# Attention and feed-forward on one core: another table of instruction order, buffer slots written out, three streamed parts of w2 in place of four

## The chip, the cores and the metric

The kernel runs on one core of a Trainium2 chip. The metric is device time in microseconds (us). Five engines run side by side, each through its own list of instructions in order: TensorE (PE, matrix products into PSUM), VectorE (DVE), ScalarE (ACT), GpSimd (POOL) and SyncE (SP), which here only issues DMA transfers. Engines wait for one another by semaphores.

## What is computed

The reference, cut to what matters: attention with random features, and then a two-layer network with an ELU between the layers.

```python
# q, k, v: [8, 8, 576, 64]; omega: [128, 64]
def phi(x):
    proj = np.einsum('bhsd,md->bhsm', x, omega)
    h = proj - np.sum(x * x, axis=-1, keepdims=True) / 2.0
    h = h - np.max(h, axis=-1, keepdims=True)
    return np.exp(h) / np.sqrt(m)
q_p, k_p = phi(q * scale), phi(k * scale)
kv, z = np.einsum('bhsm,bhsd->bhmd', k_p, v), np.sum(k_p, axis=2)
num = np.einsum('bhsm,bhmd->bhsd', q_p, kv)
den = np.einsum('bhsm,bhm->bhs', q_p, z)[..., None] + 1e-06
x = (num / den).transpose(0, 2, 1, 3).reshape(4608, 512)
h = x @ w_in                                      # w_in: 512 x 2048
g = np.where(h > 0.0, h, np.exp(np.minimum(h, 0.0)) - 1.0)
out = g @ w_out                                   # w_out: 2048 x 512
```

The weights arrive as 64-bit floats, and the kernel converts them on the chip.

## The kernel before

**Tiling.** The heads are taken two at a time, 32 pairs. For each pair the kernel loads k, q and v, projects them (`project`: the products `ppk` and `ppq`), takes minima and exponentials (`hk`, `hq`), sums k against v (`kv`), divides by the denominators (`finish`: `pz`, `den`) and multiplies (`output` or `visit`: `pn`, `pc`). The first 8 pairs are read by feature and squared on the chip (`square` in `project`); q and k of the later pairs come in a mixed layout. The tokens are nine blocks of 512. Blocks 0 and 1 run the first layer as plain products (`layer1`, tiles `ph`), in the order block 0 first half, block 1 first half, block 0 second half, block 1 second half, 32 steps F in all; while they run, the weights w1 and w2 are converted (`from_f64`, tiles `raw_w`, `u_w`) and combined (`combine`, tiles `tz`). Blocks 2 to 8 run the first layer two steps at a time as seven products in place of eight (`quad`: `pha`, `phb`, reading `w1q` tiles from memory and operands such as `A11x` or `S2x`). The second layer is `layer2` (tiles `acc`, from activations `g`, `ga`, `gb`). Numbers in a tile's name are the pair or the step F, and last a number of the buffer's.

**Visits.** For pairs 8 and up, `visit` puts the outputs of two pairs and the k-v sums of two other pairs into one stretch on PE. The sums and the last 64 tokens share one PSUM tile `pc`; ACT copies it to `zs` (L844), PE turns it (`pkt`, L847), and ACT or DVE copies that to `kvf`.

**Order.** Each operation is a numbered task of `Plan`, with the tiles that it reads and writes. `ORDER` is a table with the place of every task and, where a task may run on two engines, which one. `issue` writes the instructions in this order, so it sets each engine's list. A task of SP or ACT that issues a transfer waits in its list until its buffer is free; whatever stands behind it on that engine waits too.

**Buffers.** A tile (`Buf`) takes a buffer of its kind when its first task is issued. `SLOTS` has the number of buffers of a kind; all PSUM tiles share the kind `pa`, eight banks. w2 has 16 parts. Those named in `STREAMED` are converted once, stored to memory (`w2s`) and loaded again for each of the nine blocks into one single buffer (`w2`); the others stay in on-chip memory (`w2r`). The third piece of each `w1q` (768 KB) also has one single buffer, `w1b`; the first two pieces share three buffers.

Of the kernel before, what the change touches and what calls it, by code (L numbers as in the profile page):

```python
# [74 lines left out]
STREAMED = (3, 7, 11, 15)  # L75
# [6 lines left out]
def room(tag):  # L82
    return SLOTS[tag]
# [27 lines left out]

ORDER = """
# [189 lines left out]
class Buf:  # L302


    def __init__(self, pool, shape, dtype, tag, name, n):
        self.args, self.key, self.n = (pool, shape, dtype, name), tag, n
        self.tile, self.left, self.slot, self.listed, self.waits = None, 0, None, False, False
# [1313 lines left out]
```

## Time and profile before

| | us |
|---|---|
| median of 3 runs | 994.19 (992.09 to 994.51) |
| the profiled execution's own time | 994.99 |
| its span, first to last instruction | 992.9 |
| TensorE busy in the span | 970.7 (98%) |
| VectorE busy | 776.7 (78%) |
| ScalarE busy | 709.5 (71%) |
| GpSimd busy | 403.0 (41%) |

The profiled execution is 0.8 us above the median; 2.1 us of its time lie outside its span. Products are pipelined and the profile models their ends, so that a share of 98% leaves out short waits between products.

### The profile page before, as it was taken

What the parts mean: (1) busy time and instruction counts of PE and PEld (TensorE: products, weight loads), DVE (VectorE), ACT (ScalarE), POOL (GpSimd) and SP (SyncE); (2) the same over time, 40 slices, a digit from 0 to 9 for tenths busy, and PEclk for the clock granted to TensorE, in tenths of its full rate; (3) what the DMA queues carried; (4) which work ended last, traced back from release to release, by engine and by line L of the source; (5) the groups of instructions that cost most, each with busy time, mean ns of one, the idle gap of its engine ahead of it and who ended that gap; (6) DMA issues with size and microseconds to landing.
All of it is one profiled execution on the core that took longest, in us unless ns stands there. A gap on an engine that the chain in (4) does not pass through costs nothing.

```text
span 992.9 us, 20069 instructions
## 1 busy us (share of the span) xinstructions
PE 970.7 (98%) x6237; PEld 842.0 (85%) x6237; DVE 776.7 (78%) x2709; ACT 709.5 (71%) x1856; POOL 403.0 (41%) x382
## 2 busy tenths in 40 slices
PE   8999989999999999999999999999999999999998
PEld 7787768888778988988889988898899889898897
DVE  5999999999999978997889778787888565455343
ACT  5888867878899867896789779876998633333232
POOL 3544122245546542642555535745464322122120
PEclk8999999999999999999999999999999999999999
DMA  6767887879889888897888987887787767656763
GB/s 175 197 211 244 281 272 265 285 268 291 293 282 353 280 281 263 276 292 236 254 282 292 301 273 254 275 283 270 246 301 234 249 209 255 201 202 211 238 196 109
DMA packets 90697, 252.71 MB, mean 255 GB/s; under 512 B 11680, under 2 KB 24800, under 8 KB 90592
## 3 DMA queue, kind: packets, MB, share of 16 engines
q1 hardware_dynamic: 89648, 249.11, 77.5%
q10 hardware_dynamic: 944, 2.33, 0.8%
q8 instruction: 51, 0.84, 0.3%
q14 instruction: 54, 0.44, 0.1%
HBM read 206.83 MB, written 44.56 MB: 253 GB/s over the span
## 4 chain that ended last, share of the span: by engine, by line
PE 76%; DVE 8%; ACT 4%; DMA 3%; issue 2%; POOL 1%; DVEq 0%; ACTq 0%; POOLq 0%
PE acc L1415 35%; PE phb L1358 16%; PE pha L1358 12%; PE ppk L681 2%; PE ppq L681 2%; PE pn L817 2%; DMA w1q<-w1p 1%; PE ph L1303 1%; PE ph L1305 1%; PE ph L1304 1%; DMA xq<-in_qx_dram 1%; DVE e L1316 1%; DVE u_w L1157 1%; DVE g L490 1%; DVE u_w L1162 1%
## 5 line engine op out<-in xcount | busy, mean ns | idle before, releaser
L1415 PE MATMUL acc<-w2r,ga 128*128 128x512 f32 x504 | 136.4, 396 | 0.0
L1415 PE MATMUL acc<-w2r,gb 128*128 128x512 f32 x504 | 134.8, 395 | 0.0
L1415 PEld LDWEIGHTS acc<-w2r,ga 128*128 128x128 f32 x504 | 90.4, 189 | 16.9 <-issue 0.7
L1415 PEld LDWEIGHTS acc<-w2r,gb 128*128 128x128 f32 x504 | 90.3, 189 | 16.1
L490 POOL TENSOR_TENSOR gb<-e,gb 128x512 fp32r<-128x512 f32 x35 | 45.3, 1293 | 112.4 <-DVE gb L487 53.4
L901 DVE CUSTOM_DVE_ANT_0 junk<-hq,pz 128x128 f32<-128x128 f32 (+1 forms) x320 | 78.1, 282 | 8.9 <-PE pz L880 2.8
L690 ACT ACTIVATE p2q<-ppq,sqq 128x128 f32<-128x128 f32 x216 | 66.8, 369 | 23.3 <-PE ppq L681 17.2
L690 ACT ACTIVATE p2k<-ppk,sqk 128x128 f32<-128x128 f32 x216 | 66.4, 367 | 22.7 <-PE ppk L681 21.6
L490 POOL TENSOR_TENSOR ga<-e,ga 128x512 fp32r<-128x512 f32 x34 | 44.0, 1293 | 83.0 <-DVE ga L487 51.5
L1415 PE MATMUL acc<-w2r,g 128*128 128x512 f32 x288 | 74.5, 396 | 1.5 <-DVE mnk L699 1.2
L1387 ACT ACTIVATE e<-pha 128x512 f32<-128x512 f32 x56 | 33.5, 599 | 56.2 <-PE pha L1358 43.0
L1388 ACT ACTIVATE e<-e 128x512 f32<-128x512 f32 x112 | 70.4, 633 | 2.4
L582 ACT ACTIVATE hq<-hq,mnq 128x128 f32<-128x128 f32 x216 | 68.6, 397 | 0.2
L582 ACT ACTIVATE hk<-hk,mnk 128x128 f32<-128x128 f32 x216 | 67.8, 401 | 0.2 <-DVE mnk L699 0.2
L1367 DVE TENSOR_TENSOR phb<-phb,s 128x512 f32<-128x512 f32 x56 | 38.9, 695 | 35.1 <-PE phb L1358 34.8
L490 POOL TENSOR_TENSOR hq<-hq,den 128x512 f32<-128x512 f32 (+1 forms) x62 | 51.7, 843 | 35.8 <-DVE den L910 10.2
L699 DVE CUSTOM_DVE_ANT_0 hq<-ppq,p2q 128x128 f32<-128x128 f32 x216 | 53.1, 285 | 15.9 <-ACT p2q L690 13.9
L1415 PEld LDWEIGHTS acc<-w2r,g 128*128 128x128 f32 x288 | 52.4, 188 | 13.4 <-ACT e L1313 1.3
L490 POOL TENSOR_TENSOR tk<-xk,tk 64x576 fp32r<-64x576 f32 x33 | 47.2, 1429 | 40.6 <-DMA turned<-tb 10.0
L490 POOL TENSOR_TENSOR tq<-xq,tq 64x576 fp32r<-64x576 f32 x30 | 42.9, 1431 | 48.2 <-DVE tq L487 7.6
L699 DVE CUSTOM_DVE_ANT_0 hk<-ppk,p2k 128x128 f32<-128x128 f32 x216 | 53.1, 284 | 9.5 <-ACT p2k L690 8.4
L1390 DVE SCALAR_TENSOR_TENSOR e<-e,phb 128x512 f32<-128x512 f32 x56 | 38.2, 682 | 23.7 <-ACT e L1388 23.3
(266 smaller groups left out, 2747.6 us busy)
## 6 DMA issues: line engine op xcount, KB each, us to landing
w1q<-w1p SPq DMA_DIRECT2D x112, 512.0 KB, 5.6
w1q<-w1p SPq DMA_DIRECT2D x56, 768.0 KB, 5.5
w<-w2s SPq DMA_DIRECT2D x36, 512.0 KB, 5.9
raw_w<-in_w_dram SPq DMA_DIRECT2D x28, 512.0 KB, 4.6
xk<-in_kx_dram SPq DMA_DIRECT2D x24, 576.0 KB, 4.9
xq<-in_qx_dram SPq DMA_DIRECT2D x24, 576.0 KB, 5.5
turned<-tb SPq DMA_DIRECT2D x48, 288.0 KB, 4.2
qh<-turned SPq DMA_DIRECT2D x96, 144.0 KB, 6.0
```

The lines of the kernel that those rows point to most:

```text
L490: (nc.vector if e == "DVE" else nc.gpsimd).tensor_tensor(*args)
L582: nc.scalar.activation(h()[:, j, :], src(j), AF.Exp, bias=mn()[:, j:j + 1], scale=-1.0)
L681: nc.tensor.matmul(p()[:, a * 256:(a + 1) * 256], y()[:, o:o + P], om, start=True, stop=True)
L690: nc.scalar.activation(p2()[:, a], view()[:, a, M:], AF.Identity, bias=sq()[:, j:j + 1], scale=1.0)
L699: nc.vector.tensor_tensor_reduce(out=h()[:, j, :], in0=view()[:, a, 0:M], in1=p2()[:, a, :], scale=1.0, scalar=HIGHEST, op0=ALU.add, op1=A ...
L901: nc.vector.tensor_tensor_reduce(out=junk()[r], in0=h()[r, j, :], in1=pz()[r, a * P:(a + 1) * P], scale=1.0, scalar=EPS, op0=ALU.mult, op1 ...
L1358: nc.tensor.matmul(half(p, n), a, b, start=(first and c == 0 and i == 0), stop=(c == 1 and i == 2), skip_group_check=True,)
L1367: op("DVE", dve(n), d, lambda: nc.vector.tensor_tensor(out(), p(), x(), ALU.add), reads, writes)
L1387: op("ACT", act(TB, True), d1, lambda p=p, e=e: nc.scalar.activation(e(), p(), AF.Relu, scale=-1.0), (p,), (e,))
L1388: op("ACT", act(TB), d1 + 0.2, lambda e=e: nc.scalar.activation(e(), e(), AF.Exp, scale=-1.0), (e,), (e,))
L1390: "DVE", dve(TB), d1 + 0.8, lambda p=p, e=e: nc.vector.scalar_tensor_tensor(e(), e(), -1.0, p(), ALU.add, ALU.max),
L1415: nc.tensor.matmul(now[tt](), part_of(tt, a), w(), start=(first and n == 0), stop=(last and n == 2))
```

## The change

A new `ORDER` table; a table `SLOT` beside it, from which each tile takes the number of its buffer when its first task is ordered, where before the framework gave out the buffers of a kind in turn. Three parts of w2 are streamed, numbers 4, 9 and 15, where it was four, 3, 7, 11 and 15. The room for the thirteenth resident part comes from the tile `xc_1_3`, which now shares the buffer `w1b` with the third pieces of `w1q`. Scratch tiles `junk` become two fixed ones. The first four loads of w1 (`ASIDE`) are issued by SP, not ACT. The task costs in `op` (693 for 687 and the like) take no part in the instructions.

```diff
-STREAMED = (3, 7, 11, 15)
+STREAMED = (4, 9, 15)
...
+SLOT = """
+001010071600504023401376500203411710026275123007410026510131031140710000264621421031050561104270134020063072543111256031114035102022310063120421000143
...
 ORDER = """
-0 44 52 48 8 12 56 36 77 40 4 276 142 66 72 96 297 280 301 1004 108 100 112 144 148 68 172 176 80 84 288 152 16 104 20 284 60 500 88 24 1140 496 1008
...
+44 52 0 56 8 40 280 73 4 36 48 276 288 1004 60 284 12 96 140 69 144 66 160 148 100 104 300 78 172 152 156 176 180 1008 108 112 116 297 80 84 164 328
...
     def __call__(self):
         if self.tile is None:
             pool, shape, dtype, name = self.args
-            self.tile = pool.tile(shape, dtype, tag=self.key, bufs=self.n, name=name)
+            self.tile = pool.tile(shape, dtype, tag=self.key + self.slot, bufs=1, name=name)
         return self.tile
...
+        slots = iter("".join(SLOT.split()))
         for x in map(int, ORDER.split()):
             n, e = divmod(x, 4)
+            for b in sorted(self.tasks[n][4], key=lambda b: b.args[3]):
+                if b.slot is None:
+                    b.slot = next(slots)
...
+    junks = [const.tile([P, M], F32, name=f"junk{i}") for i in range(2)]
...
-        (blk, c): Buf(stream, [P, 2, TB], F32R, xc_tag(blk, c), f"xc_{blk}_{c}", room(xc_tag(blk, c)))
+        (blk, c): Buf(mv if xc_tag(blk, c) == "w1b" else stream, [P, 2, TB], F32R, xc_tag(blk, c), f"xc_{blk}_{c}", room(xc_tag(blk, c)))
...
-    ASIDE = ("w1_0", "w1_1", "w1_2", "w1_3")
+    ASIDE = ()
```

**The start.** SP's first issues stood so before (`xk` and `xq` are k and q of a pair, in pieces; `omf` is omega):

```order
L546 DMA xk_98<-in_k_dram 64x2x256
L546 DMA xq_100<-in_q_dram 64x2x512
L546 DMA xk_98<-in_k_dram 64x2x64
L546 DMA xq_100<-in_q_dram 64x2x64
L546 DMA xk_98<-in_k_dram 64x2x128
L546 DMA xk_116<-in_k_dram 64x2x512
L546 DMA xk_116<-in_k_dram 64x2x64
L546 DMA xq_152<-in_q_dram 64x2x64
L502 DMA omf<-in_omT_dram 64x128 x2
L546 DMA xq_152<-in_q_dram 64x2x512
L546 DMA v_164<-in_v_dram 128x650
```

and stand so now:

```order
L569 DMA xk_99<-in_k_dram 64x2x256
L569 DMA xq_101<-in_q_dram 64x2x512
L569 DMA xq_101<-in_q_dram 64x2x64
L569 DMA xk_107<-in_k_dram 64x2x64
L569 DMA xk_99<-in_k_dram 64x2x128
L569 DMA xk_99<-in_k_dram 64x2x64
L569 DMA xk_107<-in_k_dram 64x2x512
L569 DMA xq_120<-in_q_dram 64x2x64
L1162 DMA raw_w_1_122<-in_w_dram 128x1024
L569 DMA v_124<-in_v_dram 128x650
L569 DMA xq_120<-in_q_dram 64x2x512
```

The 64-column piece of the first q moved from fourth to third. The load `raw_w_1` of w1 now stands here, ninth. Before, ACT issued it, as the first rows of ACT's list show (L1522 loads its tables, L606 squares, L582 takes exponentials):

```order
L1522 ACT_TABLE_LOAD
L493 DMA of<-in_omT_dram 64x128
L544 DMA xk_98<-in_k_dram 64x2x128
L606 ACTIVATE xk_98<-xk_98 64x2x256
L1139 DMA raw_w_1_129<-in_w_dram 128x1024
L606 ACTIVATE xq_100<-xq_100 64x576
```

ACT's list now begins so:

```order
L1545 ACT_TABLE_LOAD
L516 DMA of<-in_omT_dram 64x128
L567 DMA xk_99<-in_k_dram 64x2x128
L629 ACTIVATE xq_101<-xq_101 64x576 x2
L605 ACTIVATE hk_149<-ppk_1_128,mnk_147 128x128 x4
L629 ACTIVATE xk_107<-xk_107 64x576
```

ACT squares both halves of q first; the square of the first 256 columns of k went from ACT to POOL.

**The end of block 2's first layer.** PE's products between the last use of the third piece `w1q_44_2` and the first use of the next one, `w1q_46_2`, before (the last 12 rows ahead of that first use; ahead of them stand three products of `ppk`, six of `acc` and the twelve of A11 and S2 of step 46):

```order
L1415 MATMUL acc_2_0_0_4053<-w2_43_5001,gb_42_4941 128x512
L1415 MATMUL acc_2_0_1_4039<-w2_43_5001,gb_42_4941 128x512
L1415 MATMUL acc_2_0_0_4053<-w2r_85,ga_44_5091 128x512 x2
L1415 MATMUL acc_2_0_1_4039<-w2r_85,ga_44_5091 128x512 x2
L681 MATMUL ppq_16_1_5102<-om_79,tq_16_4801 128x256 x2
L1358 MATMUL phb_46_5125<-S3x_2_3583,w1q_46_1_4865 128x256 x6
L1358 MATMUL phb_46_5125<-S1x_2_3801,w1q_46_1_4865 128x256 x6
L681 MATMUL ppq_16_0_5139<-om_79,tq_16_4801 128x256 x2
L1415 MATMUL acc_2_0_0_4053<-w2r_85,ga_44_5091 128x512
L1415 MATMUL acc_2_0_1_4039<-w2r_85,ga_44_5091 128x512
L1415 MATMUL acc_2_0_0_4053<-w2r_85,gb_44_5113 128x512 x2
L1415 MATMUL acc_2_0_1_4039<-w2r_85,gb_44_5113 128x512 x2
```

and now (ahead of them stand the twelve products of A11 and S2 of step 46, and nothing else):

```order
L1438 MATMUL acc_2_0_0_3915<-w2r_87,gb_42_4730 128x512
L1438 MATMUL acc_2_0_1_3886<-w2r_87,gb_42_4730 128x512
L1438 MATMUL acc_2_0_0_3915<-w2r_87,ga_44_4912 128x512 x2
L1438 MATMUL acc_2_0_1_3886<-w2r_87,ga_44_4912 128x512 x2
L1381 MATMUL phb_46_4928<-S3x_2_3304,w1q_46_1_4926 128x256 x6
L1381 MATMUL phb_46_4928<-S1x_2_3653,w1q_46_1_4926 128x256 x6
L1438 MATMUL acc_2_0_0_3915<-w2r_87,ga_44_4912 128x512
L1438 MATMUL acc_2_0_1_3886<-w2r_87,ga_44_4912 128x512
L1438 MATMUL acc_2_0_0_3915<-w2r_87,gb_44_4953 128x512 x2
L1438 MATMUL acc_2_0_1_3886<-w2r_87,gb_44_4953 128x512 x2
L704 MATMUL ppq_16_0_4973<-om_79,tq_16_4659 128x256 x2
L704 MATMUL ppq_16_1_4981<-om_79,tq_16_4659 128x256 x2
```

Three products of `ppk` and six of `acc` left this stretch: it held 24 products `phb` or `pha`, 18 of `acc` and seven of `ppk` and `ppq`, and now holds 24, 12 and four. On SP, ahead of the load of `w1q_46_2` stand the two stores `turned3` in both; behind it stood six fetches `qh` and the load `w2_47` before, and now five `qh`, a load of `w1q_48_0` and then `w2_47`.

**A visit.** ACT's list around the two copies `zs` in the visit of pairs 16 to 19, before:

```order
L485 CAST tq_20_6428<-xq_20_6382 64x576
L582 ACTIVATE hq_19_6251<-hq_19_6251,mnq_19_6252 128x128 x5
L844 COPY zs_19_6367<-pc_(16, 17)_(18, 19)_6393 128x128
L485 COPY xf_5_0_6459<-pn_17_6396 128x256
L844 COPY zs_18_5833<-pc_(16, 17)_(18, 19)_6393 128x128
L485 COPY xf_4_0_4889<-pn_17_6396 128x256
L485 COPY xf_5_0_6459<-pn_16_6390 128x256
L485 COPY xf_4_0_4889<-pn_16_6390 128x256
L485 CAST gb_58_6491<-e1_58_6384 128x512
L650 ACTIVATE xq_20_6382<-xq_20_6382 128x576
```

and DVE's list around its own copy out of the same PSUM tile `pc`:

```order
L901 ISA den_19_6451 128x1
L901 ISA junk_19_6_0_6455,den_19_6451<-hq_19_6251,pz_19_6431 128x128
L901 ISA den_19_6451 128x1
L901 ISA junk_19_7_1_6457,den_19_6451<-hq_19_6251,pz_19_6431 128x128
L901 ISA den_19_6451 128x1
L487 COPY xf_5_0_6459<-pc_(16, 17)_(18, 19)_6393 128x2x64
L910 RECIPROCAL den_19_6451<-den_19_6451 128x4
```

ACT's list now:

```order
L1410 ACTIVATE e1_58_6235<-phb_58_6063 128x512
L1411 ACTIVATE e1_58_6235<-e1_58_6235 128x512
L605 ACTIVATE hq_19_6056<-hq_19_6056,mnq_19_6057 128x128 x4
L508 CAST gb_58_6246<-e1_58_6235 128x512
L508 COPY xf_5_0_6248<-pn_17_6186 128x256
L867 COPY zs_18_5680<-pc_(16, 17)_(18, 19)_6183 128x128
L867 COPY zs_19_6217<-pc_(16, 17)_(18, 19)_6183 128x128
L508 COPY kvf1_81<-pkt_19_6264 128x128
L508 COPY xf_5_0_6248<-pn_16_6180 128x256
L673 ACTIVATE xq_21_6299<-xq_21_6299 128x576
L508 COPY xf_4_0_4742<-pn_16_6180 128x256
L1394 COPY s_60_6316<-pha_60_6271 128x256
```

and DVE's now:

```order
L513 TENSOR_TENSOR tq_20_6237<-xq_20_6139,tq_20_6237 64x576
L1413 SCALAR_TENSOR_TENSOR e1_58_6235<-e1_58_6235,phb_58_6063 128x512
L510 COPY xf_5_0_6248<-pc_(16, 17)_(18, 19)_6183 128x2x64
L817 TENSOR_TENSOR zr_19_6233<-zs_19_6217,zr_19_6233 128x256
L510 COPY xf_4_0_4742<-pn_17_6186 128x256
L510 CAST tq_20_6237<-xq_20_6139 64x576
L924 ISA junk0_82,den_19_6285<-hq_19_6056,pz_19_6252 64x128
```

DVE's copy out of `pc` went from behind four denominators to straight behind the add of step 58. ACT's two copies `zs` now follow each other. On PE the step 60 product `pha` follows `pkt` directly before; now four products of `acc` stand between them. In the visit of pairs 24 to 27 ACT's copy of `kvf0` stood behind four exponentials `hq_27` and a copy of `pn`; now it stands straight behind the copies `zs`.

**Choice of engines.** Over the whole program DVE has 5 instructions fewer, POOL 9 fewer and ACT 10 more. The larger moves: roundings `g` (block 0 and 1) on ACT 27 to 32, output copies `o` on ACT 24 to 28, squares of q on ACT 9 to 13, subtractions `tz` on DVE 8 to 14, normalisations `hq` on DVE 34 to 29. PE's 5649 instructions are the same ones in another order.

## Rows read from the trace of the kernel before

**Rows 1.** Busy time of each engine (instructions) by stretch, granted clock, DMA
```profile
core 0: us, PE busy (x) PEld busy (x) DVE busy (x) ACT busy (x) POOL busy (x), PEclk, DMA share, GB/s
0.00:25.00 25.00, 20.25 (x137) 19.55 (x138) 14.10 (x44) 15.00 (x44) 8.04 (x13) 0.86 0.66 176
25.00:150.00 125.00, 115.88 (x709) 93.69 (x708) 116.66 (x374) 102.89 (x274) 47.54 (x45) 1.00 0.77 242
150.00:300.00 150.00, 148.80 (x769) 120.75 (x768) 142.59 (x466) 128.29 (x326) 60.38 (x61) 1.00 0.84 282
300.00:975.00 675.00, 671.46 (x4565) 596.65 (x4564) 498.89 (x1821) 458.35 (x1208) 285.77 (x263) 1.00 0.80 258
```

**Rows 2.** What TensorE waited for, whole run: total us, times, longest
```profile
PE ppq L626 <- ACT xq L606: 2.4, 1, 2.4
...
PE pha L1358 <- DMA w1q<-w1p: 1.4, 1, 1.4
...
PE pha L1358 <- ACT kvf L485: 0.8, 1, 0.8
...
PE pkt L847 <- ACT zs L844: 0.6, 1, 0.6
```

**Rows 3.** Chain of work over 0 to 150 us: start, us, what
```profile
74.67 1.04 ACT hq L582 x4
...
118.90 0.68 DVE mnq L639
```

**Rows 4.** Timeline of the start: start, us, engine, operation, idle before
```profile
2.94 0.60 SPq L546 DMA_DIRECT2D xq<-in_q_dram  x1
...
3.79 0.36 ACTq L1139 DMA_DIRECT2D raw_w<-in_w_dram  x1
...
5.54 0.75 DVE L490 TENSOR_TENSOR xq<-xq 64x576 f32<-64x576 f32 x1 [2.51 <-DMA xq<-in_q_dram]
...
8.98 0.68 ACT L606 ACTIVATE xq<-xq 64x576 f32<-64x576 f32 x1 [4.56 <-DMA xq<-in_q_dram]
...
9.71 2.08 PE L626 MATMUL ppq<-of,xq 128*128 128x128 f32 x8 [2.39 <-ACT xq L606]
...
10.61 2.24 POOL L490 TENSOR_TENSOR xk<-xk 64x576 f32<-64x576 f32 x2 [4.06 <-DMA xk<-in_k_dram]
```

**Rows 5.** Busy time by stretch around the half clock, columns as above
```profile
10.00:15.00 5.00, 5.00 (x25) 5.00 (x25) 3.62 (x9) 2.69 (x9) 2.24 (x2) 0.50 0.79 225
15.00:20.00 5.00, 5.00 (x46) 5.00 (x46) 4.62 (x9) 4.54 (x19) 2.25 (x2) 0.99 0.82 217
```

**Rows 6.** DMA issues: count, KB each, median us to landing
```profile
w1q<-w1p SPq DMA_DIRECT2D x56, 768.0 KB, 5.5
...
xq<-in_q_dram SPq DMA_DIRECT2D x8, 32.0 KB, 3.2
```

**Rows 7.** Chain of work over 370 to 392 us
```profile
379.21 9.12 DMA w1q<-w1p
```

**Rows 8.** Chain of work over 825 to 860 us, TensorE alone
```profile
829.86 2.88 PE phb L1358 x24
...
833.46 4.20 PE acc L1415 x18
```

**Rows 9.** Timeline of ACT near 476 us
```profile
476.32 0.27 ACT L844 COPY zs<-c_(16, 17)_(18, 19)_6393 128x128 f32<-128x128 f32 x1 [1.53 <-DVE xf L487]
```

**Rows 10.** Timeline of ACT near 685 us
```profile
685.01 1.30 ACT L582 ACTIVATE hq<-hq,mnq 128x128 f32<-128x128 f32 x4
```

**Rows 11.** Groups of ACT: count, busy us, mean ns, idle before
```profile
L485 ACT CAST g<-e 128x512 fp32r<-128x512 f32 x27 | 16.8, 624 | 7.2 <-DVE e L1316 4.9 <-PE acc L1415 1.6 <-POOL g L490 0.7
...
L485 ACT COPY o<-acc 128x512 f32<-128x512 f32 x24 | 14.0, 595 | 18.9 <-PE acc L1415 16.5 <-DVE ga L490 1.5 <-POOL tz L490 0.7
```

**Rows 12.** Groups of DVE, columns as above
```profile
L490 DVE TENSOR_TENSOR hq<-hq,den 128x512 f32<-128x512 f32 x22 | 15.5, 705 | 0.2
...
L490 DVE TENSOR_TENSOR tz<-tw,tz 128x512 fp32r<-128x512 f32 x8 | 5.5, 688 | 0.2 <-ACT tz L485 0.2
```

More of the change, by code (lines that the diff above doesn't have):

```diff
@@ L306, in __init__ @@
         self.args, self.key, self.n = (pool, shape, dtype, name), tag, n
-        self.tile, self.left, self.slot, self.listed, self.waits = None, 0, None, False, False
+        self.tile, self.left, self.slot = None, 0, None
     def __call__(self):
@@ L497, in omega @@
         )
-        t = Buf(sb, [P, M], F32, "junk", "omf", 2)
+        t = Buf(sb, [P, 2, M], F32, "p2", "omf", 2)
         due += 15
@@ L501, in omega @@
             r = slice(a * D, a * D + D)
-            op("SP", 590, due, lambda r=r: nc.sync.dma_start(t()[r], omT), (), ((t, a),), D * M * 4)
+            op("SP", 590, due, lambda r=r: nc.sync.dma_start(t()[r, 0], omT), (), ((t, a),), D * M * 4)
         op(
-            "DVE", dve(M, True), due + 2, lambda: nc.vector.tensor_scalar(t(), t(), -SCALE, None, ALU.mult),
+            "DVE", dve(M, True), due + 2, lambda: nc.vector.tensor_scalar(t()[:, 0], t()[:, 0], -SCALE, None, ALU.mult),
             ((t, 0), (t, 1)), ((t, 0), (t, 1)), port=True,
         )
-        op("DVE", dve(M), due + 3, lambda: nc.vector.tensor_copy(om[:, 0:M], t()), ((t, 0), (t, 1)), ("oh",))
+        op("DVE", dve(M), due + 3, lambda: nc.vector.tensor_copy(om[:, 0:M], t()[:, 0]), ((t, 0), (t, 1)), ("oh",))
         op(
             "DVE", dve(M), due + 4,
-            lambda: nc.vector.tensor_tensor(om[:, M:], t(), om[:, 0:M].bitcast(F32), ALU.subtract),
+            lambda: nc.vector.tensor_tensor(om[:, M:], t()[:, 0], om[:, 0:M].bitcast(F32), ALU.subtract),
             ((t, 0), (t, 1), "oh"), ("om",),
@@ L633, in project @@
                     op(
-                        "PE", 223 * len(cs) + (g < 2), d + 0.01 * k, lambda cs=cs, mms=mms: mms(cs),
+                        "PE", 223 * len(cs) + 55 + (g < 2), d + 0.01 * k, lambda cs=cs, mms=mms: mms(cs),
                         [*([(x, g + 1 if g else k, 2)] if apart else [(x, a, 2) for a in range(2)]), "of"], (p,), full=1,
@@ L899, in dens @@
                 for j, a, r in slots:
-                    junk = Buf(sb, [P, M], F32, "junk", f"junk_{i}_{j}_{a}", 2)
+                    junk = junks[j % 2]
                     nc.vector.tensor_tensor_reduce(
-                        out=junk()[r], in0=h()[r, j, :], in1=pz()[r, a * P:(a + 1) * P], scale=1.0, scalar=EPS,
+                        out=junk[r], in0=h()[r, j, :], in1=pz()[r, a * P:(a + 1) * P], scale=1.0, scalar=EPS,
                         op0=ALU.mult, op1=ALU.add, accum_out=den()[r, j:j + 1],
@@ L1207, in weights @@
             fetch = (
-                "SP", 590, due - 8 + late, lambda: nc.sync.dma_start(w().bitcast(F32).rearrange("p a x -> p (a x)"), w2s[STREAMED.index(f)]),
+                "SP", 590, due - 8 + late, lambda w=w: nc.sync.dma_start(w().bitcast(F32).rearrange("p a x -> p (a x)"), w2s[STREAMED.index(f)]),
                 (("w2s", f),), ((w, "h"), (w, "l")), P * 3440,
@@ L1308, in layer1 @@
             reads = [(*k, z) for k in held(blk * TB, TB, c) for z in "hl"]
-            op("PE", 687, due + 0.5 * c, lambda c=c: mms(c), [*reads, (w, "h"), (w, "l")], (p,))
+            op("PE", 693, due + 0.5 * c, lambda c=c: mms(c), [*reads, (w, "h"), (w, "l")], (p,))
         due += 2
@@ L1458, in layer2 @@
             op(
-                "PE", 229 * len(tts) * len(which), d, lambda tts=tts, which=which: mms(tts, which),
+                "PE", 230.5 * len(tts) * len(which), d, lambda tts=tts, which=which: mms(tts, which),
                 [*((tiles[tt // 2][0], passes[n][0]) for n in which for tt in tts), *(passes[n][2] for n in which)], [now[tt] for tt in tts],
```

15 lines of the change are left out of this document (added), and 370 rows, old and new, of the table ORDER.

## The prediction

> **What bounds the kernel now.** I read the windows by stage first. [rows 1] TensorE (PE) is busy for all but 4.75 us of the first 25, 9.1 us of the next 125, 1.2 us of the 150 after, and 3.5 us from 300 to 975. A change of order that leaves PE's 5649 instructions alone can only give or take some of these idle stretches, 18.6 us together, or the time that PE spends at a lower clock. That is 2% of the whole, so the forecast is a sum of small terms.
>
> The list of PE's waits comes next. [rows 2] The longest is 2.4 us at the very start, for a square by ACT; then 1.4 us for the load of a w1q piece, 0.8 us for ACT's copy `kvf`, 0.6 us for its copy `zs`. No wait after the start is longer than a w1q load's, and none is for w2. The chain of waits shows what makes the 9.1 us: [rows 3] it runs along ACT up to about 79 us and along DVE from there to about 131 us, with PE behind them. In 25 to 150 us DVE is busy 116.66 of 125 us and ACT 102.89; in 150 to 300 us DVE 142.59 of 150 and ACT 128.29, while PE there lacks 1.2 us only. [rows 1]
>
> **The start.** ACT's square of the first q began at 8.98 us, when the 64-column piece issued at 2.94 us had landed, and PE's `ppq` began when it ended, at 9.71 us after 2.39 us of idleness. [rows 4] That landing took 6.0 us; the median of such 32 KB pieces is 3.2 us. [rows 6] The change issues this piece one place earlier, 0.60 us, so at about 2.3 us; by the median it lands at 5.5 us. ACT then squares the two halves of q (0.68 us each), and `ppq` starts near 5.5 + 1.4 = 6.9 us, 2.8 us earlier. But two fewer projections (four products) are ready ahead of that point in the new order. At 2.08 us for eight such products [rows 4] they give back 1.0 us. I take -1.8. The other end: with the same slow landing of 6.0 us, `ppq` starts at 2.3 + 6.0 + 1.4 = 9.7 us, nothing is gained, and the four products cost +1.0. The square of k's first 256 columns that went to POOL can cost no more than POOL's price for an operation on 576 columns, 1.12 us (two took 2.24) [rows 4]; PE waits for q at that place, so I take nothing for it.
>
> The load `raw_w_1` went from ACT's list to SP's ninth place. It cost ACT 0.36 us of issuing [rows 4], between its table load and the square that waited for data anyway: 0 on the path. The Trainium skill ("DMA: Bandwidth & Descriptors", section "Issuing engines are not separate DMA queues") says that transfers run on the same 16 DMA engines whoever issues them, so that a second issuing engine saves sequencer time alone. By that rule the big load would disturb q's small piece from SP's list just as from ACT's; no row here shows the same load issued from both. By it the sum keeps 0 for a changed issuer; what the later place in time may give stays in the bound of -1.8.
>
> **25 to 150 us.** I added up, for each step F, the instructions ahead of that step's add on DVE in both orders, at the mean of their groups. DVE has 2 to 5 us less to do ahead of most of the first 27 steps, and the same at step 31. The moves behind it over the whole program: five `hq` fewer at 705 ns, six `tz` more at 688 ns [rows 12], five `g` and four `o` handed to ACT, which takes 624 and 595 ns for them [rows 11]. DVE is the chain's engine from 79 us on [rows 3], so a list shorter there brings its results forward. PE can gain at most its idle 9.1 us. ACT heads the chain before 79 us and gets nothing lighter, so only the second part should gain: I take -2.5, about a quarter of the idle time and the low end of the 2 to 5 us. Ends: 0 and -9.1.
>
> **The visits.** At 476 us ACT's copy `zs_18` waited 1.53 us for DVE's copy out of the same PSUM tile [rows 9], because that copy stood behind four denominators. PE's `pkt` lost 0.6 us to it [rows 2] and the products behind about as much again. The change puts DVE's copy ahead of the denominators, ACT's two copies next to each other, and four `acc` between `pkt` and `pha`: I take -1.2. At 685 us four exponentials took 1.30 us [rows 10] ahead of the copy `kvf0`, for which PE waited 0.8 us [rows 2]; now the copy stands ahead of them: -0.8. Together -2.0. What these engines do instead is late later: four denominators and four `hq` move back about 1.2 us, and PE has no wait for them before. If the waits only change place, the end is 0.
>
> **Step 46.** The load of `w1q_46_2` was issued when the last product with `w1q_44_2` freed the single buffer, at 379.21 us, and took 9.12 us [rows 7]; PE had 7.7 us of other work and waited the rest, 1.4 us [rows 2]. From 24 products in 2.88 us and 18 `acc` in 4.20 us [rows 8] a small product costs 0.12 us and an `acc` 0.233 us. The stretch of 24 small ones, 18 `acc` and seven projections is 2.9 + 4.2 + 0.8 = 7.9 us by this, close to the 7.7 seen. The new one, with 12 `acc` and four projections, is 2.9 + 2.8 + 0.5 = 6.2 us. If the load still takes 9.1 us the wait grows to about 3.0 us, +1.6. If it takes the 5.5 us that is the median of these loads [rows 6], the wait is gone, -1.4. What surrounds it in SP's list is nearly the same, so I can't choose: 0.
>
> **Streaming and buffers: 0.** One part of w2 less to load in each block takes away nine loads and one store of 512 KB, about 5 MB. PE had no wait for w2 in the list of waits, so the cover is PE's own work: between the last use of the single buffer and the next first use I count at least 7.1 us of products before, and 9.6 us now. `xc_1_3` in the buffer of w1q's third pieces is last read 16.9 us of PE work ahead of the first piece that follows in it, more than the 9.12 us of the slowest such load [rows 7]. These distances are the product counts of the order at the prices above. What would cost: a load behind a store in SP's list, up to the 9.1 us of a load. The distances don't suggest it. Fixed slots for `junk` and tiles free no engine by themselves; the tail's order is nearly the old one.
>
> **Sum.** -1.8 - 2.5 - 2.0 + 0 + 0 = -6.3 us against the profiled 994.99, so 988.7; the median lies 0.8 us lower, so 987.9. I write 988.0, 0.6% below.
>
> **Rivals.**
> *B. The half clock goes too, and most of the early waits.* From 10 to 15 us the granted clock was 0.50, the 1.2 GHz level, and PE got through 25 products against 46 in the next 5 us at 2.4 GHz. [rows 5] 25 products need 2.7 us at the higher rate, so 2.3 us were lost, right after PE had stood idle 2.39 us. If `ppq` follows without that gap, the low clock may not come: -2.3 more, and with -6.5 in place of -2.5 for 25 to 150 us the time is 988 - 6.3 = 981.7. The Trainium skill ("TensorE: Matmul & The Clock Gate", section "HAM oscillation — how this bites in real kernels") says that an engine left waiting for data falls back to half rate and pays the return each time. This trace agrees in that the half clock stands right behind the long wait; it speaks for B. Against B: the first products are few whichever way, two fewer now, and ACT's part of the chain isn't shortened.
>
> *C. The gains are given back.* The waits move: step 46 waits 3.0 us (+1.6), the small q piece lands as late as before (0 to +1.0 in place of -1.8), and half of the rest comes back as waits elsewhere (+2.2): 988 + 1.6 + 2.3 + 2.2 = 994. For it speaks that PE at 98% has no slack to absorb a new wait; against it, that three different places improve independently.
>
> *D. Slower: ACT becomes the bound.* ACT receives five `g` and four `o`, 5 x 0.624 + 4 x 0.595 = 5.5 us [rows 11], and four squares of q at 0.68 us [rows 4], 2.7 us more: 8.2 us in all. In 150 to 300 us it is at 128.29 of 150 us [rows 1], so 22 us are free there on the mean. But it already heads the chain up to 79 us [rows 3], where a longer list arrives at PE at once. If all of it fell where ACT is behind and came through to PE, with the other gains kept by half: 995 - 3 + 8.2 = 1000. It decides once ACT's busy share in some stretch of 25 us between 25 and 300 us comes to nearly all of it. Against it: most of these moves lie behind 79 us, where DVE is the later one.
>
> That the change doesn't do what it says is no rival here: the order shows it.
>
> **How the numbers follow.** The forecast has 0.50, with its own range of 984 to 991.5 (the start between -1.8 and -4, the early stage between 0 and -5, step 46 either way). B has 0.14, C 0.20, D 0.16. A tenth below and a tenth above left out, the range is 980 to 998: it takes in B, C, and D's half. A measurement of this kernel tells about 0.3%, 3 us, from no change. Faster than 991.2: nearly all of the forecast's 0.50 and B's 0.14, less the upper edge, 0.62. Within 3 us: C and that edge, 0.21. Slower than 997.2: D, and a little of C, 0.17.
>
> **What the next profile would show.** Right: `ppq` starts near 7 us; PE idles 6 to 7 us in 25 to 150 us and DVE's busy time there is less; no wait of PE for `zs` at 476 us nor for `kvf` at 685 us; the idle time from 300 to 975 us near 1.5 us, or near 3 us if step 46 still waits. Wrong: a wait above 2 us for `w1q_46_2`; any wait for w2; ACT as releaser of PE's waits between 79 and 300 us with its busy share above 95%; or a `ppq` that still starts behind 9 us.

## The result, and the profile after

| | before | changed |
|---|---|---|
| median | 994.24 us (992.09 to 994.51) | 979.58 us (978.55 to 982.46) |
| ratio | | 0.9862, 95% interval 0.9837 to 0.9887 |
| span of the profiled execution | 992.9 us | 977.8 us |

The change is 14.7 us faster (11 to 16 us by the interval). The forecast was 988.0, and the range began at 980.0: the time lies 0.4 us below it. The windows by stage of the changed kernel (columns as in [rows 1]):

```profile
core 0: us, PE busy (x) PEld busy (x) DVE busy (x) ACT busy (x) POOL busy (x), PEclk, DMA share, GB/s
0.00:25.00 25.00, 21.90 (x151) 20.87 (x151) 15.83 (x52) 16.70 (x49) 9.51 (x15) 1.00 0.74 188
25.00:150.00 125.00, 121.53 (x742) 100.80 (x743) 119.59 (x395) 110.41 (x290) 46.20 (x42) 1.00 0.77 244
150.00:300.00 150.00, 149.87 (x840) 124.08 (x839) 142.81 (x495) 135.40 (x350) 57.56 (x57) 1.00 0.88 293
300.00:960.00 660.00, 657.10 (x4445) 583.40 (x4445) 486.76 (x1762) 449.82 (x1177) 277.80 (x258) 1.00 0.77 252
```

Read it against [rows 1]: PE's idle time fell from 4.75 to 3.1 us in the first 25, from 9.1 to 3.5 in the next 125, from 1.2 to 0.1 in the 150 after; behind 300 us it is the same few us. DVE is busier in 25 to 150 us, not less busy as the prediction's signs had it, and ACT too: both do more in the same time, as PE does (742 products, not 709). PE's longest waits now:

```profile
PE pha L1381 <- DMA w1q<-w1p: 2.3, 3, 0.8
PE ppk L649 <- POOL xk L513: 1.3, 2, 1.1
...
PE ppq L649 <- DVE e L1339: 0.7, 1, 0.7
```

The waits for `zs` and for the visits' `kvf` [rows 2] are gone. Those for w1q have grown: with one of 0.4 us in `phb` they are 2.7 us here and 1.7 us in a second trace of the changed kernel, against 1.4 us in [rows 2] and 0.8 us in a second trace of the kernel before.

PE's products are the same in all the kernels below, so that one number says how far each is behind at the same point of its work. I took the median time from one product's start to the next for each kind of product, over the nine traces of the table (the kernels are those of the experiments below; "framework's buffers" is the changed kernel without the buffer numbers, experiment 1), added these up in the order of the trace, and took the sum from the time at which the point is reached. What is left is the time that PE lost up to there, by waits or by a lower clock. The work comes to about 949 us at the end. (This is worked out from the traces, it is no view of the profile.)

```
PE work done, us      10    20    30    60   100   140   250   400   650   end
kernel before        8.4   9.4  12.0  16.9  22.0  26.7  28.7  34.4  39.2  40.9
before, again        6.1   7.4  10.0  14.9  20.0  25.3  27.5  31.2  36.0  38.5
omega's copy moved   7.7   8.3   9.4  12.7  17.1  23.4  24.8  28.4  32.9  35.1
fixed scratch        6.6   7.3   8.3  12.0  15.9  22.6  24.1  28.4  32.9  34.6
three parts          7.0   7.7   8.4  12.2  16.1  20.9  22.3  26.2  31.5  33.7
changed              5.3   7.4   8.1  11.4  13.6  15.6  16.6  19.1  23.8  25.5
changed, again       5.1   8.1   8.8  12.0  14.5  15.8  16.8  20.0  23.3  24.9
framework's buffers  4.3   5.5   6.3   9.2  11.6  13.1  14.7  17.4  22.3  23.4
same, again          4.9   6.1   7.1  10.0  13.0  15.7  16.3  18.7  22.8  23.7
```

Between 10 and 140 us of work the kernel before loses 18 to 19 us and the changed one 10.5. That is more than half of the gain; the rest is spread thin.

### The profile page after: what moved, and what is told of

The parts are those of the page before. It is cut to its first block, busy times and chain, and to the rows that moved or that the text cites. A ratio compares the mean times of both kernels' runs of the same rounds, so it can differ in the third digit from the quotient of the medians.

```text
span 977.8 us, 20075 instructions
## 1 busy us (share of the span) xinstructions
PE 964.7 (99%) x6237; PEld 840.7 (86%) x6237; DVE 768.4 (79%) x2704; ACT 716.5 (73%) x1870; POOL 394.0 (40%) x373
## 4 chain that ended last, share of the span: by engine, by line
PE 85%; DMA 7%; ACT 6%; DVE 1%; issue 1%; POOL 0%; SPq 0%; ACTq 0%; POOLq 0%
PE acc L1438 39%; PE phb L1381 15%; PE pha L1381 11%; DMA w1q<-w1p 3%; PE ppk L704 2%; PE ppq L704 2%; PE pn L840 2%; PE ph L1326 2%; PE ph L1328 2%; PE ph L1327 2%; DMA raw_w<-in_w_dram 2%; ACT hk L605 1%; ACT hq L605 1%; PE ppq L649 1%; DMA xq<-in_q_dram 1%
## 5 line engine op out<-in xcount | busy, mean ns | idle before, releaser
L1438 PE MATMUL acc<-w2r,gb 128*128 128x512 f32 x546 | 146.7, 396 | 0.2 <-DVE e L1413 0.2
L1438 PE MATMUL acc<-w2r,ga 128*128 128x512 f32 x546 | 146.5, 396 | 0.0
L1438 PEld LDWEIGHTS acc<-w2r,gb 128*128 128x128 f32 x546 | 97.9, 189 | 18.5 <-DVE gb L513 0.4
L1438 PEld LDWEIGHTS acc<-w2r,ga 128*128 128x128 f32 x546 | 97.8, 189 | 18.5 <-issue 0.5
L513 POOL TENSOR_TENSOR gb<-e,gb 128x512 fp32r<-128x512 f32 x37 | 48.3, 1305 | 126.8 <-DVE gb L510 66.8
L1438 PE MATMUL acc<-w2r,g 128*128 128x512 f32 x312 | 80.1, 396 | 0.1
L513 POOL TENSOR_TENSOR hq<-hq,den 128x512 f32<-128x512 f32 (+1 forms) x67 | 57.4, 867 | 37.1 <-DVE den L933 21.9
L1410 ACT ACTIVATE e<-phb 128x512 f32<-128x512 f32 x56 | 33.4, 596 | 48.3 <-DVE phb L1390 46.6
L1438 PEld LDWEIGHTS acc<-w2r,g 128*128 128x128 f32 x312 | 56.5, 188 | 12.1 <-DVE g L513 0.7
L513 POOL TENSOR_TENSOR tq<-xq,tq 64x576 fp32r<-64x576 f32 x27 | 38.7, 1433 | 60.2 <-DVE zr L817 8.8
```

What stands on the lines that cost most here:

```text
L513: (nc.vector if e == "DVE" else nc.gpsimd).tensor_tensor(*args)
L1410: op("ACT", act(TB, True), d1, lambda p=p, e=e: nc.scalar.activation(e(), p(), AF.Relu, scale=-1.0), (p,), (e,))
L1438: nc.tensor.matmul(now[tt](), part_of(tt, a), w(), start=(first and n == 0), stop=(last and n == 2))
```

## The experiments

The theory to begin with was the prediction's: the order and the engine choice leave DVE less to do ahead of each step. The rivals: the buffer numbers, the streaming, the start.

**1. The buffer numbers.** The changed order, with the framework's own choice of buffers:

```diff
-self.tile = pool.tile(shape, dtype, tag=self.key + self.slot, bufs=1, name=name)
+self.tile = pool.tile(shape, dtype, tag=self.key, bufs=self.n, name=name)
```

> The changed kernel with its order and its three streamed parts, but without the written-out buffer numbers: the framework gives the buffers of a kind out as before. If the order alone carries the gain, as I think, the time stays at 980 us, within 2. If the buffer numbers carry it (rival), it comes back to 990 or more.

977.44 us, ratio 0.9843 (0.9827 to 0.9859), 0.6 us below the expected 978 to 982. The written-out numbers gain nothing. Side by side once more at the end:

> The changed kernel, unchanged, beside the next one. If the written-out buffer numbers cost something, it is 1.5 us or more slower than the next. If they are worth nothing, within 1.5.

> The changed kernel with the buffers given out by the framework, beside the one ahead: 977 to 980 us, by the ratios to the kernel before 0.984 to 0.986. A version faster than both kernels only if it is clear of the one ahead by more than the two intervals.

978.65 (0.9852, 0.9836 to 0.9868) with the numbers, 976.91 (0.9835, 0.9818 to 0.9852) without. The framework's choice was ahead both times, by 1.7 and 2.1 us, but the intervals overlap: not shown to be faster.

**2. Engine choice against places.** Every task keeps its place and takes the engine of the other kernel:

```diff
-ORDER: place of the change, engine of the change
+ORDER: place of the change, engine of before
```

> The changed kernel with every task at its new place, but on the engine that it had before (340 tasks differ). The prediction saw the gain of the early stage in the engine choice, which gives DVE less to do: by that at least half of the 14.7 us is lost, 987 or more. If the places of the tasks in the lists carry the gain, it stays below 984.

> The kernel before with every task at its old place, but on the engine that the change gives it. Engine choice as the cause: 987 or less. Places as the cause: 994 within 3, or slower, since the engine was chosen for another place.

1054.7 us (1.0619, 1.0602 to 1.0636) and 1069.31 us (1.0769, 1.0754 to 1.0783). Neither expectation saw this: against the kernel before, each half alone costs 61 or 76 us; against the changed kernel, whose places it keeps, the first costs 75 to 76. The three longest entries in the first one's list of PE's waits are for POOL, and they are 13.4 us of it:

```profile
PE acc L1422 <- POOL ga L497: 6.9, 7, 2.1
PE acc L1422 <- POOL g L497: 3.4, 2, 2.5
PE ppq L633 <- POOL xq L497: 3.1, 1, 3.1
```

So engine choice and places can't be priced apart in this way; a table is one thing. The prediction's counts of tasks that changed engine, over the whole program, said little.

**3. The streaming and the scratch tiles.** The kernel before in its old order, with parts 3, 7 and 15 streamed:

```diff
-STREAMED = (3, 7, 11, 15)
+STREAMED = (3, 7, 15)
-ORDER: 5098 tasks
+ORDER: the same without the store and the nine loads of part 11
```

> The kernel before, in its old order and with its old engines, with three parts of w2 streamed (3, 7 and 15; the fetches and the store of part 11 are left out of the order, the part stays on the chip, xc_1_3 moves to the buffer of the third w1q pieces, the scratch tiles are fixed). The prediction gave streaming and buffers 0: 994 within 2. If the 5 MB less of traffic make the other loads land sooner (rival), 990 or less.

986.42 us, ratio 0.9933 (0.9919 to 0.9946): 6.7 us faster, where the prediction had 0. But this kernel holds more than one edit: the scratch tiles are fixed and `xc_1_3` has moved as well. The next one has the scratch tiles alone:

```diff
-junk = Buf(sb, [P, M], F32, "junk", f"junk_{i}_{j}_{a}", 2)
+junk = junks[j % 2]
-t = Buf(sb, [P, M], F32, "junk", "omf", 2)
+t = Buf(sb, [P, 2, M], F32, "p2", "omf", 2)
```

> The kernel before with the scratch tiles fixed and omega's half copy in a buffer of kind p2, as in the change; four parts of w2 are streamed as before. If the gain of the run with three streamed parts came from the scratch tiles (their products on DVE start 4 ns earlier, 320 of them, 1.3 us), 992 or less, at most 987. If it came from the streaming, 993 within 2.

988.62 us, ratio 0.9949 (0.9932 to 0.9966). These two edits give 5.1 us of the 6.7; the intervals of the two runs overlap, so that what three streamed parts in place of four add is not clear. Which of the two edits it is, a run with only the second of them (`omf`) says:

> The kernel before with one edit: omega's copy goes into a buffer of kind p2, and the two scratch buffers go on rotating. In the kernel before that copy holds one of the two until about 60 us, and each denominator waits for the one ahead of it (331 ns apart, not 209, for 41 of them: 5.0 us on DVE). If that is the whole of the 5.0 us of the run with fixed scratch tiles, 989.5 within 1.5. If the fixed tiles themselves matter, 992 or more.

989.97 us, ratio 0.9962 (0.9947 to 0.9977), as expected: omega's copy alone gives 3.8 us, clear of 0. The timeline of DVE shows it, each denominator's product in the kernel before:

```profile
28.17 0.28 DVE L901 CUSTOM_DVE_ANT_0 junk<-hq,pz 128x128 f32<-128x128 f32 x1
...
28.60 0.29 DVE L901 CUSTOM_DVE_ANT_0 junk<-hq,pz 128x128 f32<-128x128 f32 x1
...
29.04 0.29 DVE L901 CUSTOM_DVE_ANT_0 junk<-hq,pz 128x128 f32<-128x128 f32 x1
```

and the same ones where omega's copy is elsewhere:

```profile
26.39 0.28 DVE L901 CUSTOM_DVE_ANT_0 junk<-hq,pz 128x128 f32<-128x128 f32 x1
...
26.60 0.28 DVE L901 CUSTOM_DVE_ANT_0 junk<-hq,pz 128x128 f32<-128x128 f32 x1
...
26.83 0.29 DVE L901 CUSTOM_DVE_ANT_0 junk<-hq,pz 128x128 f32<-128x128 f32 x1
```

The duration of one is the same; the distance of the starts is 0.43 and 0.44 us against 0.21 and 0.23. These three also wait for ACT's `hq`; where the products before wait for nothing else, they start 0.33 us apart. Over the first 70 us the mean distance of 41 neighbours (starts less than 0.7 us apart) is 362 ns before, in both traces of that kernel, and 248 with the copy elsewhere. The list of instructions with their waits tells why (the second denominator of pair 0, before and with the copy elsewhere):

```
L901 ISA junk_1_1_255,den_253<-hq_207,pz_246 128x128 [waits DVE_49,Activation_49]
L901 ISA junk_1_1_255,den_253<-hq_207,pz_246 128x128 [waits Activation_49]
```

The denominators' products go into two scratch buffers in turn, which nobody reads. Omega's copy was a tile of the same kind and held one of the two until its last use. That use is at 89.80 us in the trace of before, not near 60 as I wrote in the expectation:

```profile
89.80 1.02 DVE L510 TENSOR_TENSOR om<-omf,om 128x128 fp32r<-128x128 f32 x1
```

Until then every product wrote where the one ahead of it had just written, and waited for its end. The same trace shows both distances, 0.33 us ahead of that use and 0.21 behind it:

```profile
66.26 0.29 DVE L901 CUSTOM_DVE_ANT_0 junk<-hq,pz 128x128 f32<-128x128 f32 x1
...
66.59 0.29 DVE L901 CUSTOM_DVE_ANT_0 junk<-hq,pz 128x128 f32<-128x128 f32 x1
...
91.67 0.28 DVE L901 CUSTOM_DVE_ANT_0 junk<-hq,pz 128x128 f32<-128x128 f32 x1
...
91.88 0.28 DVE L901 CUSTOM_DVE_ANT_0 junk<-hq,pz 128x128 f32<-128x128 f32 x1
```

In the groups of instructions the denominators' busy time and the idle time ahead of them, before and with the copy elsewhere:

```profile
L901 DVE CUSTOM_DVE_ANT_0 junk<-hq,pz 128x128 f32<-128x128 f32 (+1 forms) x320 | 78.1, 282 | 8.9 <-PE pz L880 2.8 <-ACT xf L485 1.0 <-ACT hq L582 1.0
```

```profile
L901 DVE CUSTOM_DVE_ANT_0 junk<-hq,pz 128x128 f32<-128x128 f32 (+1 forms) x320 | 75.2, 282 | 6.9 <-PE pz L880 2.8 <-ACT xf L485 1.0 <-ACT hq L582 1.0
```

4.9 us of DVE in all (2.9 busy, since starts that stand apart overlap less, and 2.0 idle), for 3.8 us of the kernel's time. The same wait put back into the new order:

> The changed kernel (buffers given out by the framework, 977.4 us) with only the scratch tiles put back as before: two that rotate, one of them taken by omega's copy until about 60 us. If each denominator's wait for the one ahead of it is what the fixed tiles removed, DVE's denominators in the first 70 us go back from 209 ns apart to about 330, and the time rises by 3 to 5 us. If the new order has room on DVE for that, it stays within 1.5.

980.84 us, ratio 0.9866 (0.9845 to 0.9886), 2.3 and 3.1 us over the two runs with fixed tiles and the same buffers (0.9843, 0.9835). The result lies between the two expectations and the intervals overlap, so that neither this price nor a difference to the 3.8 us of the old order is shown. The neighbours' mean distance is 322 ns again, against 248 in the changed kernel. The wide distances end with omega's copy here too: its last use is at 65.9 us, and the next neighbours, from 83.4 us, start 0.21 us apart.

**4. What the fourth part's loads cost.** In the kernel with three streamed parts, and later in the changed one, I issued nine loads twice:

```diff
-lambda w=w: nc.sync.dma_start(w()..., w2s[...])
+lambda w=w: [nc.sync.dma_start(w()..., w2s[...]) for _ in range(2 if f == 7 else 1)]
```

> The kernel before with three streamed parts (986.4 us), where each load of part 7 is issued twice: nine loads of 512 KB more, so the traffic of four parts, with the buffers, the slots and the conversions of three. If the traffic is the cause, it comes back to 992 or more. If the buffers that the change moves are the cause, it stays within 2 of 986.4.

> The changed kernel with the framework's buffers, where each load of part 9 is issued twice: the nine loads of 512 KB that the change removed are back as traffic. If they cost what they cost in the old order, +5 us against the run without them. If the new order has room for them, within 1.5.

991.62 (0.9983, 0.9968 to 0.9998) and 992.64 us (0.9990, 0.9977 to 1.0003): 5.2 and 15.7 us more. This was no clean test of traffic. The second load writes the buffer that the first is still writing, so SP stands until the first has landed, with all that is behind it in SP's list. SP's waits in the changed kernel with the double loads:

```profile
SPq L1209 <- DMA w<-w2s: 53.7, 10, 8.0
```

and in the old order with three parts:

```profile
SPq L1193 <- DMA w<-w2s: 40.2, 9, 6.1
```

In the changed kernel each us that SP stood went with 0.29 us of time, in the old order with 0.13: such a stop has no fixed price here.

A load that stands behind such a stop in the changed kernel, of k, with what DVE does when it has landed (chain of waits, 540 to 610 us; PE then waited 2.8 us for the `e` of L1391):

```profile
543.19 6.38 DMA xk<-in_kx_dram
...
550.98 0.77 DVE tk L491
551.76 0.70 DVE e L1391
```

The bytes without that stop: nine copies of the same 512 KB from memory to memory behind the same loads, which nothing waits for (they read the same bytes, but write them to memory, not to the chip).

> The changed kernel with the framework's buffers, where each of the nine loads of part 9 is followed by a copy of the same 512 KB from memory to memory, which writes no buffer of the chip and so doesn't wait for the load ahead of it. In the run with the loads issued twice SP stood 53.7 us for the first of the two to land, and the time rose by 15.7 us. If that stop on SP was the price, the time here stays within 2 of 977; if the traffic was, it is 985 or more.

> The kernel before with three streamed parts (986.4 us) and the same nine copies from memory to memory, behind the loads of part 7. If 5 MB of traffic were what the fourth part cost, it comes back to 988.6, the time with four parts and fixed scratch tiles, or above. If not, within 1 of 986.4.

980.73 (0.9858, 0.9838 to 0.9879) and 987.63 us (0.9929, 0.9912 to 0.9945). By the ratios the old order doesn't notice the bytes (0.9933 without them); the new one perhaps does, by 1.5 to 2.3 us (0.9843 and 0.9835 without), which lies between the two expectations, and the intervals overlap. (987.63 us is 1.2 over the 986.4 of the expectation; the ratio is the same.) So most of the 15.7 us was the stop on SP and not the reading of the bytes; what it costs to write them to the chip a second time wasn't tested alone.

**5. The start.** The kernel before, profiled once more, and with q's small piece issued third:

```diff
-SP: xk 64x2x256, xq 64x2x512, xk 64x2x64, xq 64x2x64
+SP: xk 64x2x256, xq 64x2x512, xq 64x2x64, xk 64x2x64
```

> The kernel before, unchanged, profiled a second time. If the late first q (landing 6.0 us after its issue, PE idle for 2.39 us at 7 to 9.7 us, half clock from 10 to 15 us) belongs to this order, it is there again. If it is chance of one execution, the small piece lands in 3 to 4 us here, PE's first lost time is 1.5 us or more smaller, and the profiled time is below 994.

> The kernel before with one issue moved: the 64-column piece of the first q goes third instead of fourth on SP, ahead of k's small piece. The prediction's first term alone: -1.8, so 991.4; with what ACT's earlier start brings later in the first 150 us, down to 989. If q's landing is set by the transfers and not by its place, 993 within 2.

993.27 us (1.0005, 0.9992 to 1.0019) and 994.06 us (1.0004, 0.9992 to 1.0016). The medians show no gain from the issue's place; the interval leaves room for 0.8 us. In the second trace of the unchanged kernel ACT squares q at 5.96 us, not at 8.98, and `ppq` follows:

```profile
5.96 0.68 ACT L606 ACTIVATE xq<-xq 64x576 f32<-64x576 f32 x1 [1.50 <-DMA xq<-in_q_dram]
...
7.14 2.34 PE L626 MATMUL ppq<-of,xq 128*128 128x128 f32 x10
```

So the 6.0 us landing of [rows 4] isn't there in every execution of this kernel. But it was no single accident either. Eight traces of this case have the small piece of q in fourth place; it took 5.3 to 6.1 us to land in three of them (before, omega's copy moved, fixed scratch) and 2.9 to 3.1 us in the other five. The twelve traces that have it in third place, the one of this experiment among them, all show 3.4 to 3.7 us. With omega's copy moved, for one, ACT's square came late again:

```profile
9.08 0.68 ACT L606 ACTIVATE xq<-xq 64x576 f32<-64x576 f32 x1 [4.64 <-DMA xq<-in_q_dram]
```

So the place may well spare the late landing, but its worth doesn't show in the median of the kernel.

The half clock from 10 to 15 us [rows 5] isn't in the second trace of the kernel before (columns as in [rows 1]):

```profile
5.00:10.00 5.00, 5.00 (x27) 4.74 (x26) 2.33 (x6) 1.42 (x4) 0.67 (x1) 1.00 0.84 215
10.00:15.00 5.00, 3.60 (x32) 3.41 (x31) 4.70 (x9) 4.85 (x18) 3.88 (x4) 1.00 1.07 274
```

The long wait at step 46 [rows 7] is gone there too: the two waits for w1q are 0.8 us together, longest 0.5, and in five more traces in the old order (omega's copy moved, fixed scratch, three parts with and without the copies, q's piece third) none is longer than 0.5.

**6. Which engine sets the early pace.** Copies that nothing reads, added to one engine's list at steps F 1 to 17 of the changed kernel (framework's buffers):

```diff
+if eng == "DVE" and 232 < at < 990:   # or "ACT"
+    count += 1
+    if count % 12 == 0: nc.vector.tensor_copy(spare, ident)
```

> The same kernel with 21 copies of 128x128 added to DVE's list, spread over the steps F 1 to 17, which nothing waits for: about 0.2 to 0.3 us each, 4 to 6 us. If DVE's list sets PE's pace in the first 150 us, the time rises by 60% or more of what they take. If ACT sets it (the slower rival), by less than 1.5 us.

> The same kernel with 20 copies of 128x128 added to ACT's list over the same steps: 0.2 to 0.3 us each, 4 to 6 us. If ACT heads the chain ahead of 79 us, as the prediction read it, the time rises by half of what they take. If DVE alone sets the pace, by less than 1.5 us.

980.1 (0.9856, 0.9835 to 0.9877) and 979.02 us (0.9849, 0.9829 to 0.9869), against 0.9843 and 0.9835 without: a rise of 1.3 to 2.1 us and of 0.6 to 1.4 us, both inside the intervals. The instructions of the added tile (duration min, median, max in ns, first and last start in us):

```profile
L1548 DVE COPY spare<-ident x21: 203/221/1229, 44.7 to 171.0; 128x128 f32<-128x128 f32 x21
```

```profile
L1548 ACT COPY spare<-ident x20: 281/300/405, 48.1 to 171.7; 128x128 f32<-128x128 f32 x20
```

That is 4.6 us on DVE (by the median) and 6.0 on ACT. In the same sums as in the table above, PE loses 9.2 and 10.2 us between 20 and 250 us of work in the two traces without copies, 12.2 us with DVE's copies and 10.7 with ACT's. By this estimate a us on DVE's list costs 0.4 to 0.65 us, a us on ACT's 0.1 to 0.25. It rests on one trace each, each the slowest of its four runs (982.82 and 982.34 us), and the two traces without copies differ by 1.0 us themselves: that DVE's list weighs more than ACT's is suggested, not shown.

**7. Early or late part of the order.** The changed order for its first 1700 tasks, the old one behind:

```diff
-ORDER: 5088 tasks of the change
+ORDER: 1700 tasks of the change, then the remaining ones as before orders them
```

> The changed kernel's order and engines for its first 1700 tasks (to the end of the plain first layer, about 300 us), and behind them the order and the engines of the kernel before. If the order gains only ahead of 300 us, 977 to 980. If the visits and step 46 of the later part are worth the 2 us of the prediction or more, 980 or more; if the later part is worth nothing but new waits for w1q, below 977.

986.1 us (0.9911, 0.9897 to 0.9926), 7 us over the runs with the changed order. That is the second branch of the expectation, but by the same sums 4 us of it arise at the seam: PE's lost time between 250 and 300 us of work is 5.7 us there and 1.6 in the changed order with the same buffers, with the longest wait of this run:

```profile
PE pha L1343 <- DVE A12x L475: 2.8, 1, 2.8
```

Two orders don't join without a cost, so this is no clean price of the later part. Behind the seam, from 400 us of work to the end, it loses about 8.5 us. In the table above the old order with three parts loses 7.5 us there and the changed kernel 6.4 and 4.9. So the later part of the order is worth 1 to 4 us by single traces, and that it is the smaller part rests on the table, not on this run.

## Why the prediction was wrong, point by point

**The sum.** It had -6.3 us; -14.7 was measured. In measured steps, from the kernel before: omega's copy out of the scratch buffers -3.8, the fixed scratch tiles -1.3 more (not clear from 0), the fourth part with its buffer moves -1.6 (not clear), the order with its engines and the other choice of streamed parts -9.0 to -9.7, and the buffer numbers +1.7 to +2.1 (not clear). The order's step was placed in time, but no run takes its moves apart.

**Step that failed first: "Fixed slots for `junk` and tiles free no engine by themselves".** It was costed at 0 in the part on streaming and buffers. The runs put 5.1 us there in the old order (0.9949, 0.9932 to 0.9966), most of it on omega's copy. The step looked at the scratch tiles as memory that nobody reads, and not at who shares their kind: the kernel before gives `omf` the key "junk", and the change moves it to "p2" (a line that the diff ahead of the prediction leaves out). The view that would have shown it is the timeline of DVE: denominators of equal duration 0.33 to 0.44 us apart ahead of 90 us and 0.21 behind it. Durations by group, which the working used, hide a wait between two short instructions.

**Step mis-sized: "25 to 150 us", -2.5.** The place was right, the size not. Between 20 and 140 us of PE's work the time lost fell from 17.3 and 17.9 us in the two traces of before to 8.2 and 7.7 in the two of the change: 9 to 10 us. Of these about 2.5 are the scratch tiles (15.1 and 15.3 us with them moved), and about 2 came with the fourth part and its buffers (13.2 us with three parts, in one trace). Some 5 are left to the order.

The engine is DVE first, as forecast, as far as PE's waits tell. Added up over the same stretch, its waits of over 0.15 us for DVE are 4.3 and 4.9 us in the two traces of before and 1.4 and 1.3 in the two of the change; those for ACT are 2.3 and 2.4 against 1.4 and 1.1. The longest of before, between 25 and 150 us, are all gone:

```profile
PE ppk L626 <- DVE xc L1037: 1.4, 1, 1.4
PE acc L1415 <- DVE mnk L699: 1.2, 1, 1.2
PE ppk L681 <- DVE xc L1037: 1.0, 1, 1.0
```

At 140 us of PE's work DVE had been busy for 145.0 us in the old order with three parts and for 140.5 in the new one (framework's buffers), 4.5 us less, inside the 2 to 5 us that the prediction counted; its idle time up to that point is 15.8 us against 12.5 to 15.6 in the four traces of the new order. So DVE's shorter list goes along with most of the 5 us. That it is their cause isn't shown: by experiment 6 it would be worth 1.8 to 2.9 us.

The prediction took a quarter of PE's idle 9.1 us because ACT heads the chain ahead of 79 us; the copies on ACT's list suggest that ACT is the weaker bound. And the idle time wasn't all that PE could gain, as the prediction had it: between 25 and 150 us it fell by 5.6 us, and the rest of the 9 to 10 was gained in stretches that the windows count as busy. The far end of the prediction's range, -9.1, was near, in part by the scratch tiles and the fourth part, which it had at 0.

**The start, -1.8: a price from one trace.** The small piece landed 3.4 us after its earlier issue, and ACT began the squares of q at 5.53 us, as the prediction had it (5.5):

```profile
5.53 1.26 ACT L629 ACTIVATE xq<-xq 64x576 f32<-64x576 f32 x2 [3.52 <-DMA xq<-in_q_dram]
```

But the late landing that this spares isn't in every execution of the kernel before, and the earlier issue alone gives nothing that the median shows (experiment 5). The new order loses less up to 10 us of work, 4.3 to 5.3 us against 6.1 to 8.4; at 20 us the changed kernel stands at 7.4 and 8.1 us against 9.4 and 7.4 before, and nothing clear is left.

**The visits, -2.0: the waits went as forecast, the gain was partly given back.** ACT's two copies `zs` now follow DVE's copy with a short wait (timeline of ACT, changed kernel; 1.53 us in [rows 9]):

```profile
459.72 0.43 ACT L867 COPY zs<-c_(16, 17)_(18, 19)_6183 128x128 f32<-128x128 f32 x2 [0.29 <-DVE xf L510]
```

PE has no wait for `zs` any more, nor for the later `kvf`. But from 400 to 650 us of work the changed kernel loses 4.7 and 3.3 us in its two traces, the one before 4.8 and 4.8, so 0.1 and 1.5 us less. In the first, two waits for w1q of 0.7 and 0.8 us took the place of the visits' waits, in the second two of 0.2 us. The prediction's end of 0, "if the waits only change place", held in one trace, and nearly its -2.0 in the other; no run prices the visits alone.

**Step 46 at 0, streaming's traffic at 0: held.** The load there lands in time in the second trace of before, and costs 0 and 0.4 us in the two traces of the change; nine copies of 512 KB cost nothing that can be measured in the old order. What the prediction named as its danger, something that stops SP's list, is real: 5.2 and 15.7 us (experiment 4).

**The rivals.** B's time of 981.7 came near, and its -6.5 for 25 to 150 us was nearer to the 9 to 10 us than the forecast's -2.5, but its half clock didn't go. The changed kernel has the low rate as well: from 5 to 10 us PE got through 23 products, as few as in [rows 5], against 44 in the next 5 us. The row shows a granted clock of 1.00 for that stretch, so that here the number of products has to be read and not that column:

```profile
5.00:10.00 5.00, 4.97 (x23) 4.97 (x24) 1.40 (x3) 3.08 (x7) 1.69 (x2) 1.00 0.74 207
10.00:15.00 5.00, 4.93 (x44) 4.80 (x43) 4.33 (x10) 3.78 (x14) 0.00 (x0) 1.00 0.62 162
```

The slow stretch came 5 us earlier and cost about as much. In the second trace of the kernel before it stands there too (27 products from 5 to 10 us, experiment 5). C didn't happen. D is refuted: ACT took on the work (135.4 us busy of 150 from 150 to 300 us, where it was 128.29) and PE's waits for ACT did not grow.

## What to carry to other kernels

When tiles share a kind, look at how long the longest-lived of them holds its buffer: a copy that is needed until late can halve a pool that a chain of short instructions rotates through. Read the distance of starts between neighbours of one kind, not only their duration: an instruction that waits for the one ahead of it looks the same in a table of means. And a wait that one trace shows may not be there in the next execution: take a second trace of the same kernel before you price it. Two terms of this prediction, at the start and at step 46, rested on such waits. The first came back in two of seven further traces, the second in none of six.

## What the runs showed that I had not expected

- DVE's denominators start 0.21 us apart when each writes to another buffer than the one ahead, and 0.33 us apart (0.43 when they wait for ACT as well) when it writes to the same one, though each lasts 0.28 us: they overlap here, and a wait for the one ahead costs more than the overlap that it takes away.
- A second load into the same buffer stops SP until the first has landed: 53.7 us of SP's time over ten waits went with 15.7 us of the kernel's in the new order, 40.2 over nine with 5.2 in the old one.
- Giving 340 of the 5088 tasks the engine of another good schedule, at the same places, costs 75 to 76 us, five times what the whole change gains.
- A load of 32 KB issued fourth at the start landed after 3 us in five traces and after 5.3 to 6.1 us in three; issued third, after 3.4 to 3.7 us in all twelve.
